# The last product of a float64 weight conversion moved to GpSimd or VectorE, its power of two to ScalarE

## The chip, the cores and the metric

One core of a Trainium2 chip runs the whole program. The metric is the device time of one execution in microseconds (us); the kernel before was timed three times. Engines are named as in the profile: PE is TensorE (PEld its weight loads), DVE is VectorE, ACT is ScalarE, POOL is GpSimd, SP is the engine that issues the transfers.

## What is computed

Three stages in a row on float32 data: block attention, a feed-forward layer with a squared ReLU, and one with a softplus.

```
scores = scale * q_c @ k_c.T ; scores -= max ; attn = exp(scores) / (sum + 1e-9)   # chunks of 64
x = attn @ v_c                                   # 2304 tokens x 512
h = x @ moe_w_in ; g = s * relu(h)**2 + b ; x = g @ moe_w_out        # 512 -> 2048 -> 512
h = x @ moe2_w_in ; g = relu(h) + log1p(exp(-abs(h))) ; return g @ moe2_w_out
```

The four weight matrices reach the chip as float64 and are turned into float32 there.

## The kernel before, in words

Every matmul runs as three products of a high and a low part (`split`: a rounded copy by ACT, line 496, and the remainder by DVE, line 505). The two products into the hidden layer (`quad`, PE line 907) use a scheme of Strassen's kind, with seven products for eight blocks; the first layer's product back is plain (`block`, PE line 1111, with DVE lines 1052 and 1079 and ACT line 1066 preparing its right side), the second layer's uses seven products again (`second_by_blocks`, PE line 1262). The attention of 18 tiles (`attention`: PE lines 724, 824 and 843 for scores, transposes and values) runs at the start and overlaps with the first quads.

The weights are converted piecewise by `convert`, 64 calls of 128x512 numbers each: 32 from `weights1` (two for each of 8 parts of the inner dimension, for each layer) and 32 from `weights2`. A call takes the two 32-bit words of each float64 apart: line 391 shifts out the exponent (DVE), line 408 rebuilds it as a float32 exponent (ACT), line 421 masks the upper mantissa bits (DVE), line 435 adds the lower word (DVE), line 449 sets the sign (DVE), and line 463 multiplies mantissa, 2^-20 and signed power (DVE). In `weights1` the converted halves are then combined by four POOL operations (`sub`, line 483, 128x256 each) and split for PE; in `weights2` of the second layer POOL combines them too, and in that of the first they are only stored.

The order of instructions on each engine is not that of the code. `Work.order` is a list scheduler: each operation has a table of engines with assumed costs (`dve`, `act`, `pool`) and a due key; at each step the operation that can start first is placed, ties within 0.02 going by the key, and where an operation names two engines the one with the earlier start gets it. So an operation with other engines or costs shifts everything that is placed after it. The assumed costs know nothing of one engine holding up another at a shared memory interface.

Of the kernel before, what the change touches and what calls it, by code (L numbers as in the profile page):

```python
# [8 lines left out]
F32 = mybir.dt.float32  # L9
F32R = mybir.dt.float32r  # L10
U32 = mybir.dt.uint32
I32 = mybir.dt.int32
AF = mybir.ActivationFunctionType
ALU = mybir.AluOpType
# [7 lines left out]
DM = H * D  # L22
# [176 lines left out]
def dve(n, fast=False, pointers=0):  # L199
    return (144 + n / (1.6 if fast else 1)) / 960 + 0.14 * pointers  # L200


def act(n, psum=False, pointers=0):
    return 0.155 + n * 0.00085 + (0 if psum else 0.035) + 0.1 * pointers


def pool(n):
    return 0.55 + n * 0.0015
# [7 lines left out]
def block_attention_two_layers(  # L216
# [36 lines left out]
    nc = tc and tc.nc  # L253
# [51 lines left out]
    def cells(spans):  # L305
        return {c for a, n in spans for c in range(a // GRAIN, (a + n - 1) // GRAIN + 1)}

    def add(engines, key, emit, deps=(), uses=(), size=0, after=(), r=(), w=()):

        deps = list(deps)  # L310
        rc, wc = cells(r), cells(w)
        for c in rc | wc:
            deps.extend(wrote.get(c, ()))
        for c in wc:
            deps.extend(read.get(c, ()))
        op = work.add(engines, key, emit, list(dict.fromkeys(deps)), uses, size, after)
        for c in rc - wc:
            read.setdefault(c, []).append(op)
        for c in wc:
            wrote[c], read[c] = [op], []  # L320
        return op
# [18 lines left out]
    def at(place):  # L340
        if place.kind in base:
            a, n = base[place.kind]
            return mem(a + place.index * n, n)
        if place.kind in spread:
            return mem(spread[place.kind][place.index], N)
        return bank[place.kind][place.index]
# [7 lines left out]
    def load(key, out, in_, size, deps=(), uses=(), after=(), r=(), w=()):  # L354
        return add(
            {"SP": 0.45},
            key,
            lambda e: nc.sync.dma_start(out=out(), in_=in_()),
            deps,
            uses,  # L360
            size=size,
            after=after,
            r=r,
            w=w,
        )
# [4 lines left out]
    def convert(ph, c, part, key, dst, uses=(), w=(), gone=()):  # L370

        chain = "f", part
        f, am = Place("f"), Place("am")
        src = lambda: (w1, w2)[ph][c, part].bitcast(U32)
        ld = load(
            key - LEAD_F,
            lambda: at(f).bitcast(U32),
            src,
            2 * P * DM * 4,
            deps=gone,  # L380
            uses=[*uses, f],
            after=turn.get(chain, ()),
        )
        turn[chain] = [ld]
        words = lambda: at(f).bitcast(U32).rearrange("p (a b) -> p a b", b=2)
        a = lambda: at(am)[:, :DM].bitcast(U32)
        m = lambda: at(am)[:, DM:].bitcast(U32)
        o1 = add(
            {"DVE": dve(DM, True)},
            key,  # L390
            lambda e: nc.vector.tensor_scalar(
                out=a(),
                in0=words()[:, :, 1],
                scalar1=20,
                scalar2=0x7FF,
                op0=ALU.logical_shift_right,
                op1=ALU.bitwise_and,
            ),
            [ld],
            [f, am],  # L400
            after=turn.get(("am", part), ()),
        )
        turn["am", part] = [o1]

        o2 = add(
            {"ACT": act(DM)},
            key,
            lambda e: nc.scalar.activation(
                out=a().bitcast(I32),
                in_=a().bitcast(I32),  # L410
                func=AF.Relu,
                scale=float(1 << 23),
                bias=-float(896 << 23),
            ),
            [o1],
            [am],
        )
        o3 = add(
            {"DVE": dve(DM, True)},
            key,  # L420
            lambda e: nc.vector.tensor_scalar(
                out=m(),
                in0=words()[:, :, 1],
                scalar1=0xFFFFF,
                scalar2=0x100000,
                op0=ALU.bitwise_and,
                op1=ALU.bitwise_or,
            ),
            [o1],
            [f, am],  # L430
        )
        o4 = add(
            {"DVE": dve(DM)},
            key,
            lambda e: nc.vector.scalar_tensor_tensor(
                out=m().bitcast(F32),
                in0=words()[:, :, 0],
                scalar=2.0**-32,
                in1=m(),
                op0=ALU.mult,  # L440
                op1=ALU.add,
            ),
            [o3],
            [f, am],
        )
        o5 = add(
            {"DVE": dve(DM)},
            key,
            lambda e: nc.vector.scalar_tensor_tensor(
                out=a(),  # L450
                in0=words()[:, :, 1],
                scalar=0x80000000,
                in1=a(),
                op0=ALU.bitwise_and,
                op1=ALU.bitwise_or,
            ),
            [o2],
            [f, am],
        )
        return add(  # L460
            {"DVE": dve(DM)},
            key,
            lambda e: nc.vector.scalar_tensor_tensor(  # L463
                out=dst(),
                in0=m().bitcast(F32),
                scalar=2.0**-20,
                in1=a().bitcast(F32),
                op0=ALU.mult,
                op1=ALU.mult,
            ),  # L470
            [o4, o5],
            [am, *uses],
            w=w,
        )

    def on(e):
        return nc.gpsimd if e == "POOL" else nc.vector
# [37 lines left out]
    def weights1(ph, i, key):  # L515

        wf, wp = Place("wf"), Place("w1")
        c1 = convert(ph, 2 * i + 1, 0, key, lambda: at(wf)[:, :DM], [wf])
        c0 = convert(ph, 2 * i, 0, key + 0.1, lambda: at(wf)[:, DM : 2 * DM], [wf])

        x = lambda n: lambda: at(wf)[:, n * 256 : (n + 1) * 256]
        hl = lambda h, a, n: lambda: at(wp)[:, h * 1792 + a * 256 : h * 1792 + (a + n) * 256]
        raw = lambda a, n: lambda: at(wf)[:, a * 256 : (a + n) * 256]
        key += 0.2
        done = split(key, hl(0, 0, 3), hl(1, 0, 3), raw(1, 3), 768, [c0, c1], [wf, wp])
        s1 = sub(key, x(4), x(0), x(1), 256, [c1], [wf], ALU.add, e="POOL")
        s3 = sub(key, x(6), x(2), x(0), 256, [c0, c1], [wf], e="POOL")
        s2 = sub(key, x(5), x(4), x(2), 256, [s1, c0], [wf], e="POOL")
        s4 = sub(key, x(7), x(3), x(5), 256, [s2], [wf], e="POOL")
        done += split(key + 0.2, hl(0, 3, 4), hl(1, 3, 4), raw(4, 4), 1024, [s1, s2, s3, s4], [wf, wp])  # L530
        return wp, done

    def weights2(ph, i, key):
# [4 lines left out]
        gone = [o for j in range(NG) for o in x_ready[0, j]] if ph == 0 else quads_done[0]  # L538
        c = [
            convert(  # L540
                ph, 2 * i + y, 1, key + 0.1 * y, lambda y=y: mem(*span[y]), (), span[y : y + 1], gone
            )
# [948 lines left out]
```

## Time and profile before

| | |
|---|---|
| median of 3 runs | 842.4 us (839.83 to 844.32) |
| time of the profiled execution | 843.61 us |
| its span, first to last instruction | 841.8 us |
| PE busy, share of the span | 798.8 us, 95% |
| DVE busy | 680.3 us, 81% |
| ACT busy | 458.6 us, 54% |
| POOL busy | 148.9 us, 18% |
| granted PE clock, mean | 0.982 |

The span leaves out 1.8 us of the profiled execution's time. Busy shares are means over stages with different limits, so the rows further down cut the span into stages: the attention until about 100 us, the first layer's quads until about 265 us, its blocks until about 478 us, the second layer's quads until about 655 us, and the second layer's product back.

### The profile page before, as it was taken

The numbers are of one execution on the slowest core, as the hardware profiler recorded it, in microseconds if no ns is written. First come the engines' busy times: TensorE is split into PE (matmuls) and PEld (weight loads), VectorE is DVE, ScalarE is ACT, GpSimd is POOL, SyncE is SP. The second block draws the span as 40 slices with busy tenths as digits, with TensorE's granted clock in tenths as the row PEclk, the third lists the DMA queues.
The fourth block names the chain that finished last, engine by engine and source line by source line (L and its number), as shares of the span: only waits on it lengthen the run. The fifth ranks groups of instructions, "written<-read, shape, count | busy, mean of one in ns | idle before, by whom it ended". The sixth has DMA issues, their size and how long they took to land. (4 is left out here: it accounts for less than half of the span.)

```text
span 841.8 us, 14448 instructions
## 1 busy us (share of the span) xinstructions
PE 798.8 (95%) x5117; PEld 776.1 (92%) x5117; DVE 680.3 (81%) x1201; ACT 458.6 (54%) x953; POOL 148.9 (18%) x162
## 2 busy tenths in 40 slices
PE   4688889999998999999999889999999999999998
PEld 3577889999998999999999888999999999999997
DVE  5799888889868788999899988878784867777865
ACT  3665555666667444443434675555554655555543
POOL 4253340111111001221233251111110000000000
PEclk8699999999999999999999999999999999999999
DMA  8565347778758724767664026657667996688851
GB/s 233 192 192 174 105 144 242 256 246 264 258 214 302 265 96 136 236 189 261 211 219 150 1 95 232 212 207 247 248 232 250 367 378 219 209 266 289 282 189 58
DMA packets 80634, 180.27 MB, mean 214 GB/s; under 512 B 9009, under 2 KB 53041, under 8 KB 79665
## 3 DMA queue, kind: packets, MB, share of 16 engines
q1 hardware_dynamic: 80560, 179.34, 62.8%
q8 instruction: 40, 0.66, 0.3%
q14 instruction: 34, 0.27, 0.1%
HBM read 111.15 MB, written 68.16 MB: 213 GB/s over the span
## 5 line engine op out<-in xcount | busy, mean ns | idle before, releaser
L483 POOL TENSOR_TENSOR mem<-mem 128x256 f32<-128x256 f32 x120 | 112.1, 945 | 421.8 <-DVE mem L463 307.2
L505 DVE TENSOR_TENSOR operands<-mem,operands 128x384 fp32r<-128x384 f32 (+4 forms) x186 | 130.5, 718 | 42.8 <-ACT operands L496 40.8
L496 ACT CAST operands<-mem 128x384 fp32r<-128x384 f32 (+4 forms) x186 | 112.3, 620 | 59.1 <-PE at L1262 35.6
L907 PE MATMUL at<-operands 128*128 128x384 f32 x624 | 121.9, 337 | 1.9 <-ACT S L929 1.3
L907 PEld LDWEIGHTS at<-operands 128*128 128x128 f32 x624 | 109.1, 188 | 4.6 <-ACT S L929 2.2
L1066 ACT ACTIVATE operands<-last,b_sb 128x384 fp32r<-128x384 f32 x96 | 58.6, 617 | 100.0 <-PE A L1111 59.1
L1111 PE MATMUL S<-operands 128*128 128x384 f32 x432 | 92.4, 338 | 4.0 <-DVE operands L1079 3.4
L1111 PE MATMUL at<-operands 128*128 128x384 f32 x432 | 90.8, 335 | 0.0
L1262 PE MATMUL S<-operands 128*128 128x384 f32 x384 | 87.1, 334 | 0.0
L1262 PE MATMUL at<-operands 128*128 128x384 f32 x384 | 87.1, 334 | 0.0
L907 PE MATMUL S<-operands 128*128 128x384 f32 x420 | 84.3, 339 | 2.3 <-ACT S L929 1.4
L1111 PEld LDWEIGHTS S<-operands 128*128 128x128 f32 x432 | 76.7, 189 | 5.6 <-DVE operands L1079 4.6
L907 PEld LDWEIGHTS S<-operands 128*128 128x128 f32 x420 | 73.9, 189 | 3.5 <-ACT S L929 2.1
L1079 DVE SCALAR_TENSOR_TENSOR operands<-last,b_sb,operands 128x384 fp32r<-128x384 f32 x96 | 61.9, 654 | 18.5 <-ACT operands L1066 18.2
L1111 PEld LDWEIGHTS at<-operands 128*128 128x128 f32 x432 | 76.7, 189 | 0.0
L939 ACT ACTIVATE mem<-S 128x384 f32<-128x384 f32 x104 | 50.6, 492 | 39.7 <-PE S L907 32.0
L505 DVE TENSOR_TENSOR operands<-last,operands 128x384 fp32r<-128x384 f32 (+2 forms) x88 | 53.9, 624 | 18.0 <-ACT operands L496 16.3
L1262 PEld LDWEIGHTS S<-operands 128*128 128x128 f32 x384 | 68.3, 188 | 0.0
L1262 PEld LDWEIGHTS at<-operands 128*128 128x128 f32 x384 | 68.3, 188 | 0.0
L907 PE MATMUL at<-last,operands 128*128 128x384 f32 x336 | 67.3, 337 | 0.4
L483 DVE TENSOR_TENSOR mem<-mem 128x384 f32<-128x384 f32 (+1 forms) x108 | 60.1, 582 | 8.7 <-ACT mem L939 7.9
L907 PE MATMUL A<-operands 128*128 128x384 f32 x300 | 61.0, 342 | 5.1 <-DVE A L483 1.9
(77 smaller groups left out, 1287.5 us busy)
## 6 DMA issues: line engine op xcount, KB each, us to landing
mem<-in_w_dram SPq DMA_DIRECT2D x64, 512.0 KB, 4.3
summed<-mem SPq DMA_DIRECT2D x168, 192.0 KB, 2.3
mem<-summed SPq DMA_DIRECT2D x30, 768.0 KB, 5.3
hid<-mem SPq DMA_DIRECT2D x96, 192.0 KB, 3.0
last<-hid SPq DMA_DIRECT2D x24, 768.0 KB, 4.4
last<-summed SPq DMA_DIRECT2D x12, 768.0 KB, 4.9
mem<-forms SPq DMA_DIRECT2D x7, 1024.0 KB, 7.6
last<-in_q_dram SPq DMA_DIRECT2D x18, 256.0 KB, 3.7
```

Source lines behind the costliest of these rows:

```text
L483: lambda e: on(e).tensor_tensor(out=out(), in0=x(), in1=y(), op=op or ALU.subtract),
L496: lambda e: nc.scalar.copy(out=hi().bitcast(F32R), in_=x()),
L505: lambda e: nc.vector.tensor_tensor(out=lo().bitcast(F32R), in0=x(), in1=hi(), op=ALU.subtract),
L907: nc.tensor.matmul(acc(dst)().rearrange("p (u c) -> p u c", u=GROUP), l[a], r[c], start=start and kk == 0 and x == 0, stop=kk == 1 and x == 2,
L939: lambda e: nc.scalar.activation(out=at(go), in_=acc(place)(), func=AF.Softplus if ph else AF.Relu),
L1066: lambda e, x=x, hi=hi: nc.scalar.activation(out=mem(*hi).bitcast(F32R), in_=mem(*x, 2 + 2 * ph), func=AF.Identity, bias=b_sb[:, 0:1],),
L1079: lambda e, x=x, hi=hi, lo=lo: nc.vector.scalar_tensor_tensor(out=mem(*lo).bitcast(F32R), in0=mem(*x, 2 + 2 * ph), scalar=b_sb[:, 0:1], in ...
L1111: nc.tensor.matmul(at(accs[d])[:, :N], l[a], r[c], start=m == 0 and z == 0, stop=m == NM - 1 and z == 2,)
L1262: nc.tensor.matmul(at(accs[d])[:, :N], l[a], r[c], start=i == 0 and y == 0, stop=i == NF - 1 and y == 2,)
```

## The change

Line 421's result, an integer mantissa, gets a new ACT operation behind it that turns it into a float32 times 2^-20. Line 435's addition accordingly uses 2^-52 for the lower word. The last operation no longer needs three factors: it becomes a plain product of two tensors, and may be placed on POOL or on DVE. In the changed file the new ACT operation stands in line 435, the addition in 444, the sign in 458 and the last product in 472; what follows has line numbers higher by 4.

```diff
+        o3 = add(
+            {"ACT": act(DM)},
+            key,
+            lambda e: nc.scalar.activation(
+                out=m().bitcast(F32), in_=m().bitcast(I32), func=AF.Copy, scale=2.0**-20
+            ),
+            [o3],
+            [am],
+        )
         o4 = add(
             {"DVE": dve(DM)},
             key,
             lambda e: nc.vector.scalar_tensor_tensor(
                 out=m().bitcast(F32),
                 in0=words()[:, :, 0],
-                scalar=2.0**-32,
-                in1=m(),
+                scalar=2.0**-52,
+                in1=m().bitcast(F32),
                 op0=ALU.mult,
                 op1=ALU.add,
             ),
...
         return add(
-            {"DVE": dve(DM)},
-            key,
-            lambda e: nc.vector.scalar_tensor_tensor(
-                out=dst(),
-                in0=m().bitcast(F32),
-                scalar=2.0**-20,
-                in1=a().bitcast(F32),
-                op0=ALU.mult,
-                op1=ALU.mult,
+            {"POOL": pool(DM), "DVE": dve(DM)},
+            key,
+            lambda e: on(e).tensor_tensor(
+                out=dst(), in0=m().bitcast(F32), in1=a().bitcast(F32), op=ALU.mult
             ),
```

In the order that results, 40 of the 64 last products stand on POOL and 24 on DVE. Of DVE's 24, 17 stand among the first layer's quads, 2 among its blocks and 5 among the second layer's quads.

DVE, the program's first rows from the first tile's maximum on, before (`mx`, `sm` are a tile's maxima and sums, `at` a bank of PSUM, `mem` the memory that holds the weights under conversion):

```order
L738 TENSOR_REDUCE mx_76<-at_70 128x8
L391 TENSOR_SCALAR mem<-mem 128x512
L760 TENSOR_SCALAR mx_76<-mx_76 128x8
L421 TENSOR_SCALAR mem<-mem 128x512
L435 SCALAR_TENSOR_TENSOR mem<-mem 128x512
L449 SCALAR_TENSOR_TENSOR mem<-mem 128x512
L463 SCALAR_TENSOR_TENSOR mem<-mem 128x512
L391 TENSOR_SCALAR mem<-mem 128x512
L421 TENSOR_SCALAR mem<-mem 128x512
L801 TENSOR_SCALAR sm_77<-sm_77 128x8
L802 RECIPROCAL sm_77<-sm_77 128x8
L435 SCALAR_TENSOR_TENSOR mem<-mem 128x512
```

The same place after the change:

```order
L742 TENSOR_REDUCE mx_76<-at_70 128x8
L391 TENSOR_SCALAR mem<-mem 128x512
L764 TENSOR_SCALAR mx_76<-mx_76 128x8
L421 TENSOR_SCALAR mem<-mem 128x512
L458 SCALAR_TENSOR_TENSOR mem<-mem 128x512
L805 TENSOR_SCALAR sm_77<-sm_77 128x8
L806 RECIPROCAL sm_77<-sm_77 128x8
L444 SCALAR_TENSOR_TENSOR mem<-mem 128x512
L742 TENSOR_REDUCE mx_78<-at_71 128x8
L764 TENSOR_SCALAR mx_78<-mx_78 128x8
L391 TENSOR_SCALAR mem<-mem 128x512
L742 TENSOR_REDUCE mx_80<-at_72 128x8
```

The first tile's reciprocal and the second and third tile's maxima now stand ahead of the second conversion's work, the addition stands behind the reciprocal, and the last product is gone from this engine.

POOL, from the last tile of the attention to the program's last operation, before (`last` is memory of the first layer's blocks and of the second layer's input):

```order
L808 TENSOR_TENSOR last_120<-last_120,sm_77 128x512
L483 TENSOR_TENSOR mem<-mem 128x256
L808 TENSOR_TENSOR last_120<-last_120,sm_79 128x512
L483 TENSOR_TENSOR mem<-mem 128x256 x72
L483 TENSOR_TENSOR last_2537<-last_2537 128x2x128 x12
L483 TENSOR_TENSOR mem<-mem 128x2x128 x6
L483 TENSOR_TENSOR mem<-mem 128x256 x24
```

After the change, the part of it around the turn from the first layer's blocks to the second layer's quads:

```order
L472 TENSOR_TENSOR mem<-mem 128x512
L487 TENSOR_TENSOR mem<-mem 128x256 x3
L487 TENSOR_TENSOR last_2579<-last_2579 128x2x128 x12
L472 TENSOR_TENSOR mem<-mem 128x512
L487 TENSOR_TENSOR mem<-mem 128x256
L487 TENSOR_TENSOR mem<-mem 128x2x128 x6
L472 TENSOR_TENSOR mem<-mem 128x512
```

The last products of 128x512 now stand between the 128x256 operations that combine the weights, and two stand between those that prepare the second layer's input.

## Rows read from the trace of the kernel before

**Rows 1.** The profile's page: span, and busy time of each engine.

```profile
span 841.8 us, 14448 instructions
...
PE 798.8 (95%) x5117; PEld 776.1 (92%) x5117; DVE 680.3 (81%) x1201; ACT 458.6 (54%) x953; POOL 148.9 (18%) x162
```

**Rows 2.** Busy time by stretch: length, engines, granted clock, DMA share, GB/s.

```profile
0.00:50.00 50.00, 31.13 (x365) 25.77 (x367) 34.61 (x68) 26.24 (x114) 18.03 (x27) 0.76 0.67 207
50.00:100.00 50.00, 43.47 (x650) 37.68 (x646) 46.08 (x91) 27.92 (x50) 22.27 (x23) 0.99 0.49 145
100.00:250.00 150.00, 146.65 (x841) 143.95 (x838) 127.47 (x211) 93.40 (x187) 27.27 (x30) 0.99 0.68 232
250.00:300.00 50.00, 47.37 (x259) 46.08 (x258) 39.33 (x67) 28.59 (x54) 3.68 (x4) 0.97 0.71 261
300.00:440.00 140.00, 140.00 (x810) 140.00 (x809) 126.85 (x215) 59.35 (x103) 31.52 (x32) 1.00 0.60 194
440.00:520.00 80.00, 73.61 (x405) 69.31 (x404) 71.89 (x129) 46.06 (x94) 28.89 (x26) 1.00 0.32 110
520.00:650.00 130.00, 129.33 (x734) 127.02 (x733) 97.61 (x171) 70.39 (x141) 17.29 (x20) 1.00 0.68 237
650.00:842.00 192.00, 187.22 (x1077) 186.28 (x1075) 136.42 (x256) 106.62 (x212) 0.00 (x0) 1.00 0.72 250
```

**Rows 3.** PE's waits: line, what it waited for, us in total, times, longest.

```profile
PE at L724 <- DMA last<-in_k_dram: 7.0, 2, 6.8
PE at L843 <- DVE last L352: 5.1, 4, 2.3
PE S L1111 <- DVE operands L1079: 3.4, 4, 1.3
PE at L824 <- DVE last L770: 2.9, 2, 2.5
PE S L907 <- ACT S L929: 2.0, 3, 0.8
```

**Rows 4.** Groups of instructions by form, the conversion's: busy us, mean ns.

```profile
L449 DVE SCALAR_TENSOR_TENSOR mem<-mem 128x512 uint32<-128x512 uint32 x64 | 48.2, 753 | 2.8 <-ACT mem L408 2.6
L435 DVE SCALAR_TENSOR_TENSOR mem<-mem 128x512 f32<-128x512 uint32 x64 | 45.6, 713 | 0.8
L463 DVE SCALAR_TENSOR_TENSOR mem<-mem 128x512 f32<-128x512 f32 x64 | 44.0, 687 | 0.9
L408 ACT ACTIVATE mem<-mem 128x512 int32<-128x512 int32 x64 | 40.2, 628 | 14.8 <-DVE mem L391 14.5
```

**Rows 5.** Groups by form, operations like the new product; a copy of attention.

```profile
L483 POOL TENSOR_TENSOR mem<-mem 128x256 f32<-128x256 f32 x120 | 112.1, 945 | 421.8 <-DVE mem L463 307.2 <-ACT operands L1066 60.5 <-DVE mem L483 21.1
L808 POOL TENSOR_TENSOR last<-last,sm 128x512 f32<-128x512 f32 x18 | 19.8, 1101 | 29.0 <-DVE sm L802 17.0 <-PE at L843 5.1 <-ACT last L748 3.5
...
L505 DVE TENSOR_TENSOR operands<-mem,operands 128x512 fp32r<-128x512 f32 x14 | 9.5, 687 | 0.0
...
L352 DVE COPY last<-at 128x512 f32<-128x512 f32 x9 | 6.2, 684 | 1.5 <-PE at L824 1.1 <-ACT S L929 0.3
```

**Rows 6.** Timeline, DVE and POOL: start us, length us, instructions merged.

```profile
33.94 1.05 POOL L808 TENSOR_TENSOR last<-last,sm 128x512 f32<-128x512 f32 x1 [0.43 <-ACT last L748]
33.98 1.29 DVE L421 TENSOR_SCALAR mem<-mem 128x512 uint32<-128x512 uint32 x1
...
450.08 3.09 POOL L483 TENSOR_TENSOR mem<-mem 128x256 f32<-128x256 f32 x3 [3.16 <-DVE mem L463]
...
451.48 1.09 DVE L1052 SCALAR_TENSOR_TENSOR last<-last,s_sb 128x384 f32<-128x384 f32 x1
```

**Rows 7.** Two lines' instructions: shortest, median and longest in ns.

```profile
L421 DVE TENSOR_SCALAR mem<-mem x64: 374/420/1293, 9.8 to 618.0; 128x512 uint32<-128x512 uint32 x64
...
L1052 DVE SCALAR_TENSOR_TENSOR last<-last,s_sb x96: 601/609/1095, 265.6 to 474.6; 128x384 f32<-128x384 f32 x96
```

**Rows 8.** Timeline, PE: values of the first, second and eighteenth tile.

```profile
20.04 1.98 PE L843 MATMUL at<-last 64*64 64x64 f32 x32 [2.25 <-DVE last L352]
...
28.71 1.97 PE L843 MATMUL at<-last 64*64 64x64 f32 x32 [0.78 <-DVE last L352]
...
98.95 1.97 PE L843 MATMUL at<-last 64*64 64x64 f32 x32
```

## Prediction, on record before the changed kernel ran

> **What bounds the kernel now.** I read the page first: PE is busy for 798.8 of 841.8 us, DVE for 81%, ACT for 54%, POOL for 18% [rows 1]. So all that a change off PE can give back lies in PE's 43 us of idle time, and the stretches show where that is [rows 2]: 18.9 us in the first 50, 6.5 in the next 50 (the attention), 3.4 from 100 to 250 and 2.6 from 250 to 300 (first layer's quads, then the way into its blocks), none from 300 to 440 (blocks), 6.4 from 440 to 520 (the turn to the second layer), 0.7 from 520 to 650, 4.8 after it. The conversions lie before 625 us. DVE is nearly full in three of these stretches: 46.08 of 50 us from 50 to 100, 126.85 of 140 in the blocks, 71.89 of 80 at the turn; ACT and POOL are full nowhere.
>
> The list of PE's waits names what ends them [rows 3]: in the attention the tiles' own chain (a DVE copy in line 352, the DVE subtraction in 770) and 7.0 us for the first tiles' transfers; in the blocks and at the turn line 1079 on DVE, 3.4 us; in the quads the seed copies of line 929 on ACT. No wait of a quad's product for converted weights (lines 496 and 505) is in the list. So the change can pay where DVE is late for PE, and cost where ACT or POOL become so.
>
> **The change, part by part.**
>
> *DVE loses 64 products of three factors*, 687 ns each, 44.0 us [rows 4]; 24 come back as plain products. No such product is in the trace; the nearest row, a 128x512 operation on two tensors in SBUF, takes the same 687 ns [rows 5], so 16.5 us come back. The bounds are that row and the addition's 713 ns [rows 4], which differ by less than 1 us in all. The new addition and sign keep their forms. Gross relief: 27.5 us.
>
> *ACT gains 64 operations*. The nearest row is line 408, an integer 128x512 activation at 628 ns [rows 4]: 40.2 us, ACT at 59%. The function differs, but I see no row that makes it dearer; another table would cost loads, and the new order holds as many table loads as the old.
>
> *POOL gains 40 products of 128x512.* Line 808 has that size, but one input is a broadcast sum: 1101 ns. Line 483 has two full inputs and half the size: 945 ns, so twice that, 1.89 us, is the upper bound [rows 5]. I take 1.4 us, nearer to the row of the same size: 56 us, POOL at 24%. That is far from full; what counts is whom it holds up.
>
> *POOL holds DVE.* The timeline shows line 421 on DVE start at 33.98, just behind a 128x512 operation on POOL, and take 1.29 us [rows 6], where its median is 0.42 [rows 7]: 0.87 us lost. Under three 128x256 operations on POOL, line 1052 takes 1.09 us [rows 6] instead of its median 0.61 [rows 7]: 0.48 lost. So each new POOL product can cost DVE up to 0.87 us where it saved it 0.687. Full stops would be 40 x 0.87 = 35 us, more than the gross relief of 27.5. DVE does not lose it when it is idle or at work of another kind, so I take half, 17 us: DVE is relieved by some 10 us over the whole program, not by 44. The scheduler's costs hold no such loss.
>
> The Trainium skill speaks against such a move: GPSIMD Engine Reference, section Engine selection, puts elementwise work on VectorE because a two-input operation is about twice as slow on GpSimd; by that a product would take some 1.37 us, an estimate from the page's ratio and DVE's row, which leaves the sum as it is. The same page, section Specifications, says that GpSimd's SBUF interfaces are shared with VectorE, with contention where a DVE instruction has two SBUF inputs or a two-port mode; the rows above agree with the contention, and show less lost than the whole POOL operation (0.87 of 1.05 us).
>
> *The first 100 us.* By the order, DVE's queue down to the eighteenth tile's reciprocal loses four last products (2.75 us), four 128x512 copies that now go to ACT (4 x 684 ns, 2.74 us [rows 5]), and one addition and one sign that stand later (1.47 us); three smaller operations come in, some 1.4 us together (bounded by 0.69 each). Net 5.6 us less. Three new POOL products stand there, 2.6 us of holds at most, half taken: 4.3 us remain. DVE is busy for 81% of these 100 us, so I let 81% of that reach the tiles: the last tile's values, at 98.95 us now [rows 8], come 3.5 us earlier. One quad product fewer stands before them on PE, which is only work put off: six matmuls at 173 ns (140 us for 810 in the blocks [rows 2]), 1.0 us. Term: **-2.5 us**. Bounds: nothing reaches PE and the longer conversion delays a tile's chain by a POOL product (+2), or all 5.6 us do and the early tiles gain (see the first rival, -6).
>
> *The quads.* About 28 conversions lie in the first layer's quads. Their new ACT work, 17.6 us, lifts ACT from 93.4 of 150 us to some 71%, with a few copies going the other way to DVE. Seeds wait in that queue. Taking their delay to grow as busy over idle share (1.63 to 2.45), the 2.0 us of PE's seed waits [rows 3] become 3.0: **+1.0 us**. Bounds: 0 and +5.
>
> *Blocks and turn.* Fourteen of the sixteen products there go to POOL: 9.6 us off DVE, holds of 12.2 at most, 11 at a DVE that is 91% busy. DVE gains nothing and loses 1 to 2 us out of 13 idle ones; PE idles nowhere from 300 to 440. At the turn two POOL products stand between the operations that prepare the second layer's input. I take **0**, with bounds -4 (line 1079's 3.4 us [rows 3] and a little of the seeds) and +4 (two products of up to 1.89 us in that chain).
>
> Sum: -2.5 + 1.0 + 0 = -1.5 us. The profiled execution took 843.6 us (span 841.8 and 1.8 around it), so it would take 842.1; it lay 1.2 us above the median of the runs shown, which goes to 842.4 - 1.5 = **840.9 us**.
>
> **The rivals.**
>
> *Real relief (faster).* The attention is a chain of short steps through DVE's queue. In the new order the first tile's reciprocal no longer stands behind the second conversion's lines 391 and 421 (one of which POOL stretched), and the second tile's values may come well before the present 28.71 us [rows 8]. If all 5.6 us of the start reach PE, less 1.0 put off, and line 1079's 3.4 us go too, it is -8.0: 834.4 us. For it: DVE at 92% from 50 to 100 us, and DVE as the named releaser in rows 3. Against it: the holds.
>
> *Weights late (slower).* Each conversion's chain grows by an ACT step (0.63) and by the slower product (1.4 less 0.69), 1.3 us; the two of a part share POOL, so the part is ready 2 to 3 us later. POOL's combining operations wait for just this last product, 307 us of their idle time ends with it [rows 5], so the delay is passed on in full. There are 14 parts after the attention. If PE ends up waiting half a us for each, it is +7: 847.9 us or, with the start's gain lost too, some 849. It decides where a part's split stands less than 2 to 3 us ahead of its first product. Against it: no such wait in the list now.
>
> *DVE held for the whole of POOL's work.* If a POOL product stopped DVE for its full 1.4 us, 56 us would replace 27.5: DVE would carry 28 us more, about 6 of them in 50 to 100 and at the turn, where it is full: +5, 845.9 us. Rows 6 show less than that, so I hold it for unlikely.
>
> **How the numbers follow.** About 0.5%, 4.2 us, is what a measurement of this kernel can tell from no change. My forecast, within that: 0.46. Real relief: 0.29, faster. Weights late 0.18 and the full hold 0.07: slower by over 0.5% in most of it; 0.01 of it would still read as same. So faster 0.29, same 0.47, slower 0.24. The range reaches from somewhat beyond the first rival to beyond the second: 832 to 850 us. The forecast's own range is 837 to 845.
>
> **What would show it.** Right, if the profile after has the new ACT line at about 0.63 us, 40 POOL products at 1.2 to 1.9 us, DVE's total only some 5 to 15 us lower in spite of 27.5 removed (the copies that come over to it count too), more lines 421, 391, 1056 and 1083 stretched, and the eighteenth tile's values 2 to 5 us earlier. Wrong towards faster, if DVE drops by over 20 us and PE's waits at the turn vanish. Wrong towards slower, if PE waits for lines 500 and 509 at quad products, or POOL becomes the releaser of PE's waits. What could upset all of it is the new order itself: every operation after the first is placed anew, and a few us of PE idle time can come or go at places that no row points to.

## The result, and the profile after

The changed kernel takes 847.87 us (median of 7 runs, 846.14 to 850.14) against 839.83 us for the kernel before (median of 7, 839.21 to 844.32): ratio 1.0083, 95% interval 1.0065 to 1.0101. The ratio is that of the means. The change is slower by about 0.8%, where 840.9 us and no change were forecast: a loss of some 7 us instead of a gain of 1.5, and a time outside the forecast's own 837 to 845 us. The forecast stood on three runs with a median of 842.4 us; from the seven it would have been 838.3. The profiled execution of before took 843.6 us and lay above both medians of that kernel, with a granted clock of 0.76 in its first 50 us [rows 2]; after, it is 0.90. So the start of the two traces is not compared below without care.

The page of the changed kernel, span and busy time by engine:

```profile
span 846.1 us, 14578 instructions
...
PE 799.0 (94%) x5117; PEld 774.3 (92%) x5117; DVE 679.3 (80%) x1172; ACT 485.4 (57%) x1006; POOL 210.8 (25%) x202
```

PE's work is the same as in [rows 1]. DVE has lost 64 three-factor products and got back 24 plain ones, some 27 us less, and yet its busy time has gone down by 1 us only. So its other instructions became longer, apart from copies: eleven more of them came over than left, some 5 us in all. The stretches of [rows 2], after:

```profile
0.00:50.00 50.00, 31.99 (x418) 25.77 (x419) 33.71 (x72) 29.29 (x121) 23.82 (x32) 0.90 0.78 223
50.00:100.00 50.00, 45.46 (x614) 38.79 (x613) 44.42 (x87) 31.42 (x58) 20.86 (x22) 0.97 0.49 150
100.00:250.00 150.00, 145.16 (x820) 142.20 (x821) 118.64 (x195) 101.41 (x202) 47.25 (x44) 1.00 0.66 219
250.00:300.00 50.00, 44.37 (x241) 43.32 (x240) 40.06 (x71) 29.16 (x55) 3.92 (x4) 0.93 0.76 277
300.00:440.00 140.00, 140.00 (x810) 139.95 (x808) 132.81 (x207) 63.16 (x112) 52.85 (x46) 1.00 0.59 190
440.00:520.00 80.00, 73.13 (x402) 69.08 (x401) 74.71 (x124) 47.72 (x97) 36.65 (x31) 1.00 0.33 111
520.00:650.00 130.00, 127.61 (x723) 124.99 (x721) 95.61 (x163) 74.97 (x149) 25.41 (x25) 1.00 0.68 234
```

The striking row is 300 to 440, the first layer's blocks: DVE is busier than before (132.81 against 126.85 us) with 8 instructions fewer; the new order has a part in that, for with the instructions of before it shows 132.9 us too (run e4_new_order, in the next section). From 250 to 300 PE has lost 3.0 us. The waits of PE, as in [rows 3], show what stands there:

```profile
PE at L728 <- DMA last<-in_k_dram: 6.2, 2, 5.1
PE S L1115 <- ACT operands L1070: 5.4, 2, 5.2
PE S L1115 <- DVE operands L1083: 3.1, 5, 0.9
...
PE at L847 <- DVE last L352: 2.4, 3, 0.8
...
PE at L828 <- POOL mem L472: 1.9, 1, 1.9
```

A wait of 5.2 us at the way into the blocks is new, the attention's waits for line 352 are shorter (2.4 against 5.1 us [rows 3]), one of 1.9 us is now for POOL's product itself, and line 1083 on DVE still ends 3.1 us of waits, all but a little of it at the blocks' end. No wait of a quad product (line 911) for converted weights is in the list. The groups by form, with those that the change made or stretched:

```profile
L1056 DVE SCALAR_TENSOR_TENSOR last<-last,s_sb 128x384 f32<-128x384 f32 x96 | 71.1, 771 | 1.5 <-DMA last<-hid 1.5
L1083 DVE SCALAR_TENSOR_TENSOR operands<-last,b_sb,operands 128x384 fp32r<-128x384 f32 x96 | 70.9, 741 | 9.8 <-ACT operands L1070 9.8
L472 POOL TENSOR_TENSOR mem<-mem 128x512 f32<-128x512 f32 x40 | 61.3, 1531 | 242.5 <-DVE mem L444 214.2 <-DMA forms<-mem 25.4 <-DVE operands L1083 3.0
...
L435 ACT ACTIVATE mem<-mem 128x512 f32<-128x512 int32 x64 | 40.2, 629 | 6.2 <-DVE mem L421 6.2
L391 DVE TENSOR_SCALAR mem<-mem 128x512 uint32<-128x512 uint32 x64 | 32.1, 502 | 11.1 <-POOL mem L472 8.0 <-DMA mem<-in_w_dram 2.6
...
L472 DVE TENSOR_TENSOR mem<-mem 128x512 f32<-128x512 f32 x24 | 16.6, 692 | 0.8
```

Lines 1056 and 1083 do what these two did before:

```profile
L1079 DVE SCALAR_TENSOR_TENSOR operands<-last,b_sb,operands 128x384 fp32r<-128x384 f32 x96 | 61.9, 654 | 18.5 <-ACT operands L1066 18.2
L1052 DVE SCALAR_TENSOR_TENSOR last<-last,s_sb 128x384 f32<-128x384 f32 x96 | 59.5, 643 | 0.0
```

Their means have gone from 643 and 654 ns to 771 and 741; the medians have not moved (line 1056: 611 against 609 [rows 7]), so a few instructions became much longer. Line 391, the first step of a conversion, has a wait that the prediction did not name: 8.0 us until POOL's product has read the one buffer that all conversions share.

### The profile page after: what moved, and what is told of

The parts are those of the page before. It is cut to its first block, busy times and chain, and to the rows that moved or that the text cites. A ratio compares the mean times of both kernels' runs of the same rounds, so it can differ in the third digit from the quotient of the medians.

```text
span 846.1 us, 14578 instructions
## 1 busy us (share of the span) xinstructions
PE 799.0 (94%) x5117; PEld 774.3 (92%) x5117; DVE 679.3 (80%) x1172; ACT 485.4 (57%) x1006; POOL 210.8 (25%) x202
## 5 line engine op out<-in xcount | busy, mean ns | idle before, releaser
L487 POOL TENSOR_TENSOR mem<-mem 128x256 f32<-128x256 f32 x120 | 109.2, 920 | 123.5 <-DVE mem L472 75.8
L472 POOL TENSOR_TENSOR mem<-mem 128x512 f32<-128x512 f32 x40 | 61.3, 1531 | 242.5 <-DVE mem L444 214.2
L1083 DVE SCALAR_TENSOR_TENSOR operands<-last,b_sb,operands 128x384 fp32r<-128x384 f32 x96 | 70.9, 741 | 9.8 <-ACT operands L1070 9.8
L487 DVE TENSOR_TENSOR mem<-mem 128x384 f32<-128x384 f32 (+1 forms) x108 | 65.7, 635 | 8.6 <-ACT mem L943 4.4
L1056 DVE SCALAR_TENSOR_TENSOR last<-last,s_sb 128x384 f32<-128x384 f32 x96 | 71.1, 771 | 1.5 <-DMA last<-hid 1.5
```

The costliest lines, as they stand in the source:

```text
L472: lambda e: on(e).tensor_tensor(out=dst(), in0=m().bitcast(F32), in1=a().bitcast(F32), op=ALU.mult),
L487: lambda e: on(e).tensor_tensor(out=out(), in0=x(), in1=y(), op=op or ALU.subtract),
L1056: lambda e, x=x: nc.vector.scalar_tensor_tensor(out=mem(*x, 2 + 2 * ph), in0=mem(*x, 2 + 2 * ph), scalar=s_sb[:, 0:1], in1=mem(*x, 2 + 2 * ...
L1083: lambda e, x=x, hi=hi, lo=lo: nc.vector.scalar_tensor_tensor(out=mem(*lo).bitcast(F32R), in0=mem(*x, 2 + 2 * ph), scalar=b_sb[:, 0:1], in ...
```

## The experiments

Ratios are to the kernel before, run on the same chip. Conversions are counted in the order of the code, 0 to 63. What some expectations call the second layer's blocks are conversions 32 to 47, weights of the second layer's product back. Their work runs in the stage of the first layer's blocks (line 1115), the "quads' turn" of those texts.

### Parts of the change, each with the order that the planner gives it

No POOL (label e1_no_pool):

```diff
-            {"POOL": pool(DM), "DVE": dve(DM)},
+            {"DVE": dve(DM)},
```

> The change with its last product on VectorE alone; the new ScalarE step stays. If POOL's products cost the time (they hold VectorE and keep the one conversion buffer longer), it falls to 838 to 842 us. If the new ScalarE step does, it stays at 846 to 850. If a new order of any kind costs it, it lies anywhere from 840 to 850, since the order differs from both.

Measured 851.26 us, 1.0119 (1.0095 to 1.0142).

No ACT step (e2_no_act; edit shown against the changed kernel): the power of two goes into the exponent's bias, so that the product is the same.

```diff
-                bias=-float(896 << 23),
+                bias=-float(916 << 23),
...
-                in_=m().bitcast(I32), func=AF.Copy, scale=2.0**-20
...
-                scalar=2.0**-52,
-                in1=m().bitcast(F32),
+                scalar=2.0**-32,
+                in1=m(),
```

> The change without its ScalarE step: the power of two goes into the exponent's bias (916 in place of 896), the last product stays a plain one on POOL or VectorE. If POOL's products cost the time, 846 to 850 us. If the ScalarE step does, 838 to 842. If a new order of any kind costs it, 840 to 850 again.

Measured 850.08 us, 1.0104 (1.0074 to 1.0133). Neither part alone is faster than both, but each run has an order of its own, so they tell nothing yet. The next runs hold the order fixed.

### Order and instructions apart

The changed instructions, the same 40 products on POOL, in the order of before (e3_old_order; the ACT step is issued right behind line 421):

```diff
-            lambda e: nc.vector.tensor_scalar(out=m(), ...)
+            mantissa,      # line 421, then the new ACT step
...
-            lambda e: nc.vector.scalar_tensor_tensor(out=dst(), ...)
+            lambda e: on("POOL" if n in ON_POOL else "DVE").tensor_tensor(out=dst(), ...)
```

> The order of before kept to the last instruction, with the changed instructions put into it: the ScalarE step behind line 421, and the last product on POOL for the same 40 conversions that the change puts there. If the new order costs the time, it stays at 838 to 842 us. If the instructions do (POOL's or ScalarE's), it is at 847 us or above, since nothing in this order allows for them.

The instructions of before in the order of the change (e4_new_order):

```diff
-            lambda e: nc.scalar.activation(... scale=2.0**-20),
+            lambda e: None,
...
-            lambda e: on(e).tensor_tensor(out=dst(), ...)
+            lambda e: nc.vector.scalar_tensor_tensor(out=dst(), ...)
```

> The order of the change kept, with the instructions of before in it: no ScalarE step, all 64 last products of three factors on VectorE at the place where the change has them. If the new order costs the time, 846 to 850 us. If POOL's or ScalarE's instructions do, 836 to 842.

The instructions of before in the order of e1_no_pool (e7_e1_order, the same edit there):

> The order that results with the ScalarE step and no POOL (that of the run without POOL), with the instructions of before in it. If that order is poor in itself, 848 to 852 us, as with its own instructions. If the ScalarE step costs the time, 838 to 843.

e3_old_order: 861.93 us, 1.0259 (1.0233 to 1.0285). e4_new_order: 841.82 us, 1.0014 (1.0000 to 1.0028). e7_e1_order: 850.73 us, 1.0123 (1.0097 to 1.0149). So the change's order costs 0.1% by itself, and the order of e1_no_pool costs 1.2%, all of what that run had lost: it says nothing on POOL. PE's waits in e7_e1_order show one place where it does:

```profile
PE at L914 <- DVE mem L490: 6.6, 4, 5.7
```

### The two parts, one at a time, in either order

In the order of before: the ACT step with all products on DVE (e8_old_order_act), and 40 products on POOL without the ACT step (e9_old_order_pool).

```diff
-            lambda e: on("POOL" if n in ON_POOL else "DVE").tensor_tensor(
+            lambda e: on("DVE").tensor_tensor(
```

> The order of before, with the ScalarE step put in behind line 421 and the last product, now of two tensors, on VectorE for all. With both steps this order took 861.9 us. If the ScalarE step is the larger part of that (its hand-over to and from ACT's queue stops VectorE's queue twice in a conversion), 850 to 857 us. If POOL's products are, 841 to 846.

```diff
-            nc.scalar.activation(out=m().bitcast(F32), in_=m().bitcast(I32), ... scale=2.0**-20)
-                bias=-float(896 << 23),
+                bias=-float(916 << 23),
```

> The order of before, without the ScalarE step (the power of two in the exponent's bias), with the same 40 last products on POOL. If POOL's products are the larger part of the 861.9 us, 851 to 858. If the ScalarE step is, 841 to 846.

The same two in the change's order (e11_new_order_act, e12_new_order_pool):

> The change in its own order, with the ScalarE step but all 64 last products (of two tensors) on VectorE, at the places where the change has them. With the instructions of before this order took 841.8 us, with the change's 847.9. If the 6 us are POOL's, 841 to 843; if they are the ScalarE step's, 846 to 849. In the order of before the step cost 14 us; this one was made with it, so it should cost less.

> The change in its own order, with its 40 last products on POOL and without the ScalarE step (the power of two in the exponent's bias). If the 6 us are POOL's, 845 to 849 us; if they are the ScalarE step's, 839 to 843. In the order of before POOL's products cost 4 to 5 us.

| | order of before | order of the change |
|---|---|---|
| instructions of before | 1 | 1.0014 (1.0000 to 1.0028) |
| ACT step alone | 1.0168 (1.0143 to 1.0192) | 1.0022 (1.0010 to 1.0035) |
| 40 products on POOL alone | 1.0058 (1.0032 to 1.0085) | 1.0081 (1.0057 to 1.0105) |
| both | 1.0259 (1.0233 to 1.0285) | 1.0083 (1.0065 to 1.0101) |

The times are 854.44, 845.15, 842.94 and 848.80 us for the four new ones. The ACT step, with products of two tensors, costs 14 us in an order that was not made for it, and under 1 us in one that was. In e8_old_order_act, ACT's waits show how: the step stands where its input is not there yet, up to 7.0 us long, and the seeds behind it stand too:

```profile
ACT mem L432 <- DVE mem L424: 41.0, 46, 7.0
```

PE's waits in the same run list those seeds with 6.4 us for one kind of product alone:

```profile
PE at L913 <- ACT S L935: 6.4, 7, 2.2
```

In the change's order nearly the whole loss comes with POOL's products. Two controls: POOL work that helps nobody, and orders for the same work.

Before, with two products of 128x256 on a spare tile on POOL behind each of the same 40 conversions (e10_idle_pool; added work that nothing reads):

```diff
+            if n in ON_POOL:
+                for _ in range(2):
+                    nc.gpsimd.tensor_tensor(out=spare, in0=spare, in1=spare, op=ALU.mult)
```

> The kernel before, all its products on VectorE, and behind each of the same 40 last products two products of 128x256 on POOL on a spare tile that nothing waits for. The hold on VectorE alone is added, and POOL's own queue grows. If the hold is what POOL's products cost, 845 to 852 us. If it is the longer way of the conversion through POOL and its buffer, 840 to 843.

Measured 852.75 us, 1.0147 (1.0119 to 1.0174). DVE's busy time rises from 680.3 to 703.2 us with not one instruction more: 22.9 us of hold, 0.57 for each pair. Not all of the 12 us need be hold: POOL's queue grows too, and PE waits once, for 4.6 us in the attention, for one of its combining operations.

Before, with the planner told that the last product costs 0.02 us more, and less (e5_cost_up, e6_cost_down):

```diff
-            {"DVE": dve(DM)},
+            {"DVE": dve(DM) + 0.02},
```

> The instructions of before, with the scheduler told that the last product takes 0.02 us longer: another order, nothing else. If orders for the same work differ as much as the change moved the time, it lies anywhere from 838 to 850 us; if they do not, 839 to 842. The order of the change with these instructions took 841.8, that of the run without POOL 850.7.

> The same with the last product 0.02 us shorter in the scheduler's table. The same readings: 838 to 850 us if the order by itself moves the time so far, 839 to 842 if not.

Measured 838.94 us, 0.9978 (0.9960 to 0.9996), and 841.25 us, 1.0002 (0.9986 to 1.0017). Orders for the same instructions lie 2 us below to 10 us above the first one (with e4_new_order and e7_e1_order).

### Hold or buffer, and where

The stage that line 1115 marks, first to last start of its first product, is the place (line, shortest, median and longest in ns, first and last start in us). The changed kernel:

```profile
L1115 PE MATMUL S<-operands x432: 333/334/689, 273.0 to 478.7; 128*128 128x384 f32 x144
```

The same order with all products on DVE, e11_new_order_act:

```profile
L1115 PE MATMUL S<-operands x432: 334/334/689, 270.2 to 471.5; 128*128 128x384 f32 x144
```

205.7 against 201.3 us. PE's groups by line (busy us, mean ns, idle us ahead and what ended it) say where the 4.4 us are, first the changed kernel, then e11_new_order_act:

```profile
L1115 PE MATMUL S<-operands 128*128 128x384 f32 x432 | 93.6, 339 | 8.6 <-ACT operands L1070 5.4 <-DVE operands L1083 3.1
...
L1115 PE MATMUL S<-operands 128*128 128x384 f32 x432 | 92.1, 338 | 6.0 <-ACT operands L1070 5.2 <-DVE operands L1083 0.7
```

The idle time has grown by 2.6 us, nearly all of it ended by line 1083 on DVE, and the busy time by 1.5. What DVE did from 270 to 440 us in the changed kernel, by form:

```profile
L1056 DVE SCALAR_TENSOR_TENSOR last<-last,s_sb 128x384 f32<-128x384 f32 x86 | 63.1, 767 | 0.7 <-DMA last<-hid 0.7
L1083 DVE SCALAR_TENSOR_TENSOR operands<-last,b_sb,operands 128x384 fp32r<-128x384 f32 x79 | 57.6, 733 | 9.8 <-ACT operands L1070 9.8
...
L391 DVE TENSOR_SCALAR mem<-mem 128x512 uint32<-128x512 uint32 x17 | 10.6, 625 | 2.4 <-POOL mem L472 2.4
...
L472 DVE TENSOR_TENSOR mem<-mem 128x512 f32<-128x512 f32 x2 | 1.4, 688 | 0.0
```

And in e11_new_order_act:

```profile
L1056 DVE SCALAR_TENSOR_TENSOR last<-last,s_sb 128x384 f32<-128x384 f32 x87 | 56.1, 675 | 0.8 <-DMA last<-hid 0.8
L1083 DVE SCALAR_TENSOR_TENSOR operands<-last,b_sb,operands 128x384 fp32r<-128x384 f32 x83 | 55.2, 668 | 11.5 <-ACT operands L1070 11.4
...
L472 DVE TENSOR_TENSOR mem<-mem 128x512 f32<-128x512 f32 x16 | 10.9, 682 | 0.0
```

Leaving 14 products to POOL takes 9.5 us from DVE. Lines 1056 and 1083 get longer by 86 x 92 + 79 x 65 ns = 13.0 us, 0.93 us for each product, and the buffer's wait adds 2.4. So DVE comes out of the stretch later than if it had done the products itself, 4 of line 1083 behind; the stage's later start, 2.8 us, accounts for one or two of them. The same can be followed start by start. Counted from the stage's start in either trace, line 1056 runs 0.1 us behind e11_new_order_act after 40 us, 1.8 behind after 105, 2.7 after 147 and 4.5 at its end; PE stays within 0.1 us until its first wait past 440 us and ends 4.4 behind. Four runs separate hold from buffer and this stage from the rest; all but the last keep the change's order.

Conversions 32 to 47 take turns between the shared buffer and a tile that stands unused then (e13_two_buffers):

```diff
+        buf = lambda: mem(AT_T, 1024) if side.get(n) else at(am)
-        a = lambda: at(am)[:, :DM].bitcast(U32)
-        m = lambda: at(am)[:, DM:].bitcast(U32)
+        a = lambda: buf()[:, :DM].bitcast(U32)
+        m = lambda: buf()[:, DM:].bitcast(U32)
```

> The changed kernel in its own order, but the sixteen conversions of the second layer's blocks take turns between two buffers (the one of before and one whose tile stands unused then), so that the first step of a conversion no longer waits until GpSimd has read the buffer of the conversion before. In the changed kernel that wait is 2.4 us of VectorE's idle time between 270 and 440 us. Theory 'hold' (VectorE's two-input operations are slowed beside GpSimd's product: 767 against 675 ns for 86 of them and 733 against 668 ns for 79 in that stretch, 13 us in all against the 9.6 us that leaving the products saves): the wait goes, 1 to 2 us come back at most, 845.5 to 848. Rival 'buffer' (the conversion chain behind the kept buffer is what comes late): the 6 us come back, 842 to 844.

POOL keeps only the 15 products of conversions 32 to 47 (e14_pool_blocks), or only the 25 others (e15_pool_others):

```diff
-            lambda e: on(e).tensor_tensor(
+            lambda e: on(e if 32 <= n < 48 else "DVE").tensor_tensor(     # e14_pool_blocks
+            lambda e: on("DVE" if 32 <= n < 48 else e).tensor_tensor(     # e15_pool_others
```

> The changed kernel in its own order, with GpSimd computing only the 15 products of the second layer's blocks that it had (the other 25 on VectorE). The first matmul and the last matmul of the quads' turn lie 205.7 us apart in the changed kernel and 201.3 us where all products are on VectorE. Theory 'hold': nearly the whole loss sits there, 846 to 848, with 205 to 206 us between these two. Rival 'buffer and start' (the loss is spread over the chain of all 40): 843.5 to 845, and 202 to 203.5 us.

> The changed kernel in its own order, with GpSimd computing only the 25 products outside the second layer's blocks, those of the blocks on VectorE. Theory 'hold' (GpSimd's product costs where VectorE has no slack, in the blocks, and nothing elsewhere): 842 to 844, with 201 to 202 us between the first and the last matmul of the quads' turn. Rival 'buffer and start': 845 to 847.

Planned anew, with POOL allowed outside conversions 32 to 47 only (e16_plan_others):

```diff
-            {"POOL": pool(DM), "DVE": dve(DM)},
+            {"DVE": dve(DM)} if 32 <= n < 48 else {"POOL": pool(DM), "DVE": dve(DM)},
```

> The changed kernel with the planner allowed to give GpSimd any last product but those of the blocks, planned anew. Theory 'hold': no 4 us in the blocks (201 to 203 us between the first and the last matmul of the quads' turn), and the time is that of an order for the same work, 839 to 846. Rival 'buffer and start': 845 to 850, with the waits behind the conversion buffer as in the changed kernel.

| | time, us | ratio | line 1115's stage, us |
|---|---|---|---|
| e4_new_order, no POOL product | 841.82 | 1.0014 (1.0000 to 1.0028) | 201.1 |
| e11_new_order_act, none | 842.94 | 1.0022 (1.0010 to 1.0035) | 201.3 |
| e15_pool_others, 25 elsewhere | 842.30 | 1.0035 (1.0021 to 1.0050) | 201.5 |
| e14_pool_blocks, 15 here | 846.73 | 1.0079 (1.0054 to 1.0105) | 206.0 |
| e12_new_order_pool, all 40 | 848.80 | 1.0081 (1.0057 to 1.0105) | 205.2 |
| e13_two_buffers, all 40 | 847.24 | 1.0081 (1.0053 to 1.0109) | 205.8 |
| changed kernel, all 40 | 847.87 | 1.0083 (1.0065 to 1.0101) | 205.7 |

In this order the loss follows the 15 products. PE's groups by line show it too: in e14_pool_blocks

```profile
L1119 PE MATMUL S<-operands 128*128 128x384 f32 x432 | 93.9, 340 | 8.7 <-ACT operands L1074 5.4 <-DVE operands L1087 3.1
```

and in e15_pool_others, with the waits that DVE ends down to those of a stage without POOL's products, and line 1060 (1056 in the changed kernel) at most 0.5 us behind e11_new_order_act from 50 us into the stage to its end:

```profile
L1119 PE MATMUL S<-operands 128*128 128x384 f32 x432 | 92.2, 338 | 6.0 <-ACT operands L1074 5.2 <-DVE operands L1087 0.8
```

The buffer is not the cause. In e13_two_buffers no wait for POOL is left on DVE in this stretch, and nothing came back: the conversion's first steps now run beside POOL's product. These three lines are 1.9 us longer than in the changed kernel and the conversion's second step is 0.6 longer, about the 2.4 us that the wait had been.

```profile
L1068 DVE SCALAR_TENSOR_TENSOR last<-last,s_sb 128x384 f32<-128x384 f32 x86 | 63.8, 773 | 0.8 <-DMA last<-hid 0.8
L1095 DVE SCALAR_TENSOR_TENSOR operands<-last,b_sb,operands 128x384 fp32r<-128x384 f32 x79 | 58.2, 740 | 9.9 <-ACT operands L1082 9.9
L398 DVE TENSOR_SCALAR mem<-mem 128x512 uint32<-128x512 uint32 x17 | 11.2, 657 | 0.0
```

e16_plan_others missed: 851.87 us, 1.0148 (1.0127 to 1.0168), the stage 207.8 us, against 839 to 846 and 201 to 203. Two last runs ask why, and what POOL's products outside the blocks are worth in a good order: the order of e16_plan_others with the instructions of before (e17_plan_others_old, edit as in e4_new_order), and the order of e5_cost_up with 25 plain products on POOL outside conversions 32 to 47 and no ACT step (e18_good_order_others, edit as in e9_old_order_pool).

> The order of the run planned anew without the blocks' products on GpSimd (851.9 us), with the instructions of the kernel before: no added step on ScalarE, every last product of three factors on VectorE. If that order is poor in itself, 849 to 853. If GpSimd's 25 products or the added step cost it, 840 to 845.

> The order of the fastest run so far (the planner told that the last product costs 0.02 us more; 838.9 us), without the added step on ScalarE (its power of two goes into the exponent's bias) and with 25 products outside the second layer's blocks as plain products on GpSimd, the others plain products on VectorE. Theory 'hold': nothing lost where VectorE has slack and nothing gained either, 838 to 841. If the relief of VectorE outside the blocks is worth something: 835 to 837.5, faster than both kernels. If GpSimd's products cost there too: 842 to 846.

e17_plan_others_old: 849.67 us, 1.0100 (1.0079 to 1.0121). Two thirds of that loss are the order's own. e18_good_order_others: 841.35 us, 1.0017 (0.9991 to 1.0043): not better than e5_cost_up without POOL, rather 0.4% worse (the two intervals only just overlap). So that these 25 products cost nothing is not shown beyond the change's order, where they cost 0.13%. The fastest kernel of the study is e5_cost_up, which holds nothing of the change.

## Why the prediction was wrong

**The step that failed** is "Blocks and turn: I take 0". It set 11 us of holds against 9.6 of relief, and let the 1 to 2 us that are left disappear in "13 idle ones". In place of 0 the stage grew by 4.4 us, just beyond the bound of +4, and the whole time by 0.48% (changed kernel less e15_pool_others) to 0.57% (e14_pool_blocks less e11_new_order_act), 4 to 5 us. Both sizes in that term were off.

The holds came to 13.0 us and a buffer wait of 2.4, more than the 12.2 called the most. That bound used 0.87 us, lost beside an operation of 1.05 us, for products that were taken at 1.4. The traces show a hold that goes with the length of POOL's operation. In the changed kernel 43 instructions of lines 1056 and 1083 are longer than 0.64 us; each starts while a POOL operation runs, and loses the time that this has still to run, less 0.19 to 0.20 us. Behind line 472 that is 0.86 to 1.04 us, 14 times, 14.2 us in all over the stage; behind the 128x256 operations of line 487 it is 0.47 to 0.49, 29 times (28 in e11_new_order_act). The row behind the 0.87 reads the same way: line 421 started 0.04 us behind an operation of 1.05 us [rows 6], so 0.87 was lost of 1.01 us left.

And the 13 idle us were those of before's order [rows 2]. The change's order packs this stage tighter: with the instructions of before it keeps DVE busy for 132.9 of the 140 us from 300 to 440, and the stage takes 201.1 us, where the order of before took 207.1. (Some 2 of these 6 us are two quad products that stand in the stage before; 3.3 are shorter waits of PE.) Most of the idle time that is left there is DVE's wait for ACT's line 1070 (11.4 us from 270 to 440 in e11_new_order_act), and 9.8 us of it are still idle in the changed kernel, so little of it took up the lag. The lag shows as PE's waits past 440 us. The changed kernel's timeline has a late hold and a late wait: the POOL product of a conversion, beside it line 1083, which takes 1.65 us instead of its median 0.61, and 17 us on a wait of PE for a later instruction of that line.

```profile
454.50 2.21 POOL L472 TENSOR_TENSOR mem<-mem 128x512 f32<-128x512 f32 x1 [4.63 <-DVE mem L444]
...
455.48 1.65 DVE L1083 SCALAR_TENSOR_TENSOR operands<-last,b_sb,operands 128x384 fp32r<-128x384 f32 x1
...
472.55 0.62 PE L1115 MATMUL S<-operands 128*128 128x384 f32 x2 [0.77 <-DVE operands L1083]
```

That one hold does not make the wait; most of the lag is older.

That slack matters fits e9_old_order_pool, though less cleanly: in the order of before, the same products lengthen lines 1055 and 1082 to 702 and 770 ns in the mean from 270 to 440 us (639 and 644 before), and the waits that line 1082 ends grow by 1.1 us only (4.5 against 3.4 [rows 3]), where the change's order has 2.4 more. The stage stays at 207.1 us there, but the two executions differ in their clock: from 270 to 280 us the granted clock is 0.83 in the mean in the trace of before, part of it at the lower level of 1.2 GHz, and 1.00 in this one. With holds and no relief (e10_idle_pool) those waits are 7.1 us, and the stage is 211.3 us in that order too.

**DVE's ledger** was right in direction: 27.5 us of relief, mostly eaten by holds. Its total fell by 1 us, not by 5 to 15; the copies that came over, 5 us, count in it. Within the change's order DVE's busy time is 682.3 us with no product on POOL, 675.9 with the 25 elsewhere, 686.5 with the 15 of the blocks and 679.3 with all. At 0.69 us of relief each, the 25 held DVE by 0.43 us apiece, just the half of 0.87 that was taken, and the 15 by 0.97. So the same move relieves DVE in one stage and loads it in another. Lines 421 and 391 were named among those that would stretch; 391's mean went from 473 to 502 ns, but 421's fell from 579 to 484. The Trainium skill (GPSIMD Engine Reference, section Engine selection) puts such a product on VectorE, as GpSimd takes about twice as long; the trace agrees (median 1.376 us on POOL, 0.692 on DVE), and so does the price in the blocks, 1.0079 (e14_pool_blocks) against 1.0022 (e11_new_order_act).

**The first 100 us** (-2.5 us). The eighteenth tile's values start at 94.35 us after, against 98.95 [rows 8]. But seven executions of this order, with or without the change's instructions, have them between 91.9 and 97.1 us, three more of the order of before (e8_old_order_act, e9_old_order_pool, e10_idle_pool) between 96.4 and 99.2, and the granted clock of the first 50 us differs between executions. The direction fits; the size can't be told from these, and no run pair shows a gain in the whole time.

**The quads** (+1.0 us). The ACT step took 629 ns, as taken, and cost 0.0008 of the time in the change's order, 0.7 us, which is less than the intervals tell apart. That holds only for an order that plans it.

**POOL's product** has a median of 1.376 us (1.4 taken) and a mean of 1.531.

**The rivals.** "Weights late" has the measured time, 847.9 us, by luck; it has not the mechanism: no quad product waits for lines 500 or 509, and the ACT step, which was part of its longer chain, costs nothing that shows here. "DVE held for the whole of POOL's work" was given 0.07 and is nearest to what happened: the 14 instructions of lines 1056 and 1083 that a product held lost nearly all of what it still had to run. Not every product held one, so in the blocks it came to 0.93 us of the 1.74 that a product took (24.4 us for 14). That rival looked for the loss from 50 to 100 us and at the turn, not in the blocks. "Real relief" fell: line 1083's waits stayed.

**The warning on the new order** was half right. This order costs 0.1% in sum; it loses 5.2 us at the way into the blocks, a wait that e4_new_order has too, and gets 3.3 us of that back by shorter waits in the blocks, as long as POOL stays out of them. Summed in this order: order 0.14%, ACT step 0.08%, 25 products elsewhere 0.13% (e15_pool_others less e11_new_order_act) and 15 in the blocks 0.57% (e14_pool_blocks less the same) give 0.92%, where 0.83% was measured; the intervals of the single runs are wider than the difference.

What stays open: why e16_plan_others loses another 0.5% to its instructions (in its profiled execution the granted clock is 0.91 from 440 to 520 us, where e17_plan_others_old has 1.00, and PE is busy for 802.6 us against 798.8; both idle for some 2 us from 460 to 470 us, where the clock begins to fall in the one, so what brought it down is not shown), and where e9_old_order_pool loses 0.6%, of which its blocks show some 1 us (its profiled execution was the fastest of its ten).

## What to carry to other kernels

Work moved to an engine whose operations hold up those of the one it relieves, as POOL's do here, is priced by the hold: compare the stretched neighbours with the instruction that was saved, in the stage where the relieved engine has least slack. Read that slack from the order in which the new work will stand; a scheduler that packs a stage tighter takes away idle time that was to hide the cost. And before a part of such a change is credited or blamed, run its order with the old instructions: orders for the same work differed here by up to 12 us.

## What the hardware showed beyond that

A 128x512 product on POOL held one DVE instruction for up to 1.04 us. Shortest, median and longest of line 1056, changed kernel:

```profile
L1056 DVE SCALAR_TENSOR_TENSOR last<-last,s_sb x96: 603/611/1651, 271.7 to 476.0; 128x384 f32<-128x384 f32 x96
```

and e11_new_order_act, where POOL has only operations of 128x256 beside it, up to 0.49:

```profile
L1056 DVE SCALAR_TENSOR_TENSOR last<-last,s_sb x96: 601/609/1096, 268.9 to 468.8; 128x384 f32<-128x384 f32 x96
```

Both engines can be the one that is held. In the quads of the changed kernel line 509 takes 2.07 us behind a product that started 0.3 us ahead of it and ran its 1.29, and 1.23 us where it started first; there the product takes 2.27.

```profile
217.58 1.29 POOL L472 TENSOR_TENSOR mem<-mem 128x512 f32<-128x512 f32 x1 [1.63 <-DVE mem L444]
217.88 2.07 DVE L509 TENSOR_TENSOR operands<-mem,operands 128x1024 fp32r<-128x1024 f32 x1
...
243.32 1.23 DVE L509 TENSOR_TENSOR operands<-mem,operands 128x1024 fp32r<-128x1024 f32 x1
243.43 2.27 POOL L472 TENSOR_TENSOR mem<-mem 128x512 f32<-128x512 f32 x1 [2.90 <-DVE mem L444]
```

POOL's product took 1.74 us in the mean from 270 to 440 us, where DVE is full, 1.40 in e15_pool_others, which keeps them out of there, and once, at 411 us, 3.58.

```profile
411.04 3.58 POOL L472 TENSOR_TENSOR mem<-mem 128x512 f32<-128x512 f32 x1 [4.82 <-DMA forms<-mem]
```
